# Decode attention with a gated FFN: scores keep the queries stationary on four quadrants, the softmax runs along the free axis, and one permutation matmul brings the probabilities back

## The chip, the cores and the metric

The kernel runs on one NeuronCore of a Trainium2 chip. The metric is device time in microseconds (us) of one execution. In the profile the engines are PE (TensorE, matmuls), PEld (its weight loads, which overlap with matmuls), DVE (VectorE), ACT (ScalarE), POOL (GpSimd) and SP (SyncE, which issues the loads). L371 is line 371 of the kernel before.

## The reference

One decode step for 8 sequences: attention over a sliding window of cached keys and values, multiplied by a gate from a GEGLU FFN.

```python
xn = _layernorm(x)                                   # x: 8 x 1 x 512
q  = (xn @ wq)                                       # 32 heads of 128
k  = k_cache[:, :, 3072:4096, :]                     # 8 sequences, 8 kv heads, last 1024 keys
v  = v_cache[:, :, 3072:4096, :]                     # each kv head serves 4 query heads
p  = softmax(q . k * 128 ** -0.5)                    # over the 1024 keys
s  = (p . v).reshape(B, 1, 4096) @ wo                # 4096 -> 512
g  = silu((gelu(xn @ w_gate) * (xn @ w_up)) @ w_down)
out = x + s * g
```

All inputs are bf16: 47.4 MB are read (33.6 MB of keys and values, 4.2 MB each of `wq` and `wo`, 5.5 MB of FFN weights), and 8 KB are written.

## The kernel before

**Groups and sets.** A group is one sequence with one kv head: 1024 keys, 1024 values, 4 query heads. There are 64 groups, in 16 sets of four (`QG = 4`; the four groups of a set are four sequences with the same kv head). One load brings the keys of a set, one the values, 1 MB each, so that partition e*4+g holds 32 keys of group g that lie next to each other in memory: each partition reads 8 KB in one piece, and every 128-key column block c has 32 keys of each of the four groups, interleaved on the partitions.

**Loads.** All loads are issued by SP in the order written (L159 to L173): FFN weights, `wq`, the keys of `LAG = 2` sets, and then for each set q the keys of set q+2, the values of set q and, for every second set, 0.5 MB of `wo`. They go into a ring of 16 buffers of 1 MB (`wo` has its own space). SP issues a load when its buffer is free.

**Before the sets.** The layernorm, the FFN and the query projection run while the first keys are on their way; `keep_busy` puts in matmuls that nobody reads, to keep TensorE working.

**One set.** The order on every engine is the order in which the program is written (L508 to L531). The loop runs over q (sets) and i (the four quarters of a set). In quarter i it emits the transpositions of the next quarter (`transposes`, L364: eight 128x128 blocks of K to PSUM, then two copies to SBUF, five blocks by VectorE, L371, and three by ScalarE, L373), the scores of this quarter (`scores`, L393: eight matmuls with kT as the stationary operand and the 16 query columns of the set as the moving one; each key meets the queries of all four groups, and the mask matmul L382 puts -1e30 on the three that are not its own), and a quarter of the values of set v = q - `LAG` (`values`, L472).

**Softmax before.** Scores lie as keys on partitions, 32 column blocks x 16 queries on the free axis. The maximum over a set's keys takes a reduction over blocks (L404), a transposition on TensorE (L412), a second reduction (L414), two small operations that put the negated maximum in two bf16 parts on a diagonal (L419, L422), and a matmul that adds it to all scores (L433). ScalarE takes the exponential (L442) and writes `pT`, keys on partitions, as the values need it. The sums over keys are eight matmuls with ones (L447), a reduction (L455) and a reciprocal (L461). `normalise` (L483) scales the output of a set.

**End.** `project` (L498) multiplies four heads by their part of `wo` for each second set; the last four heads come after the loop, followed by the gate, four transpositions, the addition of x, and the store.

PSUM has eight banks: two for K's transposition, two for scores, one each for maxima, sums, values and the rest.

Of the kernel before, what the change touches and what calls it, by code (L numbers as in the profile page):

```python
# [9 lines left out]
ALU = mybir.AluOpType  # L10
# [7 lines left out]
def kernel(  # L18
# [28 lines left out]

    nc = tc.nc
# [21 lines left out]
    AC = 3  # L70
# [4 lines left out]
    QC = QG * rep  # L75
    SH = B // QG
    LAG = 2
# [7 lines left out]
    p_pool = ctx.enter_context(tc.tile_pool(name="p_pool", bufs=4))  # L85
    small = ctx.enter_context(tc.tile_pool(name="small", bufs=2))
    ps_misc = ctx.enter_context(tc.tile_pool(name="ps_misc", bufs=1, space=PSUM))
    ps_kT = ctx.enter_context(tc.tile_pool(name="ps_kT", bufs=2, space=PSUM))
    ps_sc = ctx.enter_context(tc.tile_pool(name="ps_sc", bufs=2, space=PSUM))
    ps_mx = ctx.enter_context(tc.tile_pool(name="ps_mx", bufs=1, space=PSUM))  # L90
    ps_sum = ctx.enter_context(tc.tile_pool(name="ps_sum", bufs=1, space=PSUM))
# [5 lines left out]
    qT_all = persist.tile([P, B, Hq], BF16, name="qT_all")  # L97
# [70 lines left out]
    for q in range(NQ):  # L168
# [23 lines left out]
    nc.vector.memset(ones_pp, 1.0)  # L192

    row_of = consts.tile([QG, P // QG, QG], BF16, name="row_of")
    nc.vector.memset(row_of, 0.0)
    nc.gpsimd.affine_select(
        out=row_of,
        in_=row_of,
# [3 lines left out]
        pattern=[[0, P // QG], [1, QG]],  # L202
        channel_multiplier=-1,
    )
    other = consts.tile([QG, QG, rep], BF16, name="other")
    nc.vector.memset(other, MASK)
    nc.gpsimd.affine_select(
        out=other,
        in_=other,
        compare_op=ALU.not_equal,  # L210
        fill=0.0,
        base=0,
        pattern=[[1, QG], [0, rep]],
        channel_multiplier=-1,
    )

    LO = 32
    diag = []
    for i in range(2):
        t = consts.tile([LO + QC, QC], BF16, name=f"diag{i}")  # L220
        nc.vector.memset(t, 0.0)
        diag.append(t)
# [131 lines left out]
    nc.vector.tensor_copy(out=qT_all, in_=qT_ps.rearrange("p h b -> p b h"))  # L354


    kT, sc, pT, mxs, shift, recip = {}, {}, {}, {}, {}, {}

    def transposes(g):
# [9 lines left out]
        own = (NSC - AC) * P  # L369
        ta = kT_pool.tile([P, own], BF16, name="kTa")  # L370
        nc.vector.tensor_copy(out=ta, in_=kT_ps[:, 0:own])  # L371
        tb = kT_pool.tile([P, W - own], BF16, name="kTb")
        nc.scalar.copy(out=tb, in_=kT_ps[:, own:])  # L373
        kT[g] = [ta[:, c * P : (c + 1) * P] for c in range(NSC - AC)]
        kT[g] += [tb[:, c * P : (c + 1) * P] for c in range(AC)]

    def scores(g):
        q, i = divmod(g, NB)
        hkv, b = divmod(q * QG, B)
        if i == 0:  # L380
            sc[q] = ps_sc.tile([P, NCS, QC], FP32, name="sc_ps")
            nc.tensor.matmul(  # L382
                sc[q],
                row_of.rearrange("g e s -> g (e s)"),
                other.rearrange("g s j -> g (s j)")
                .unsqueeze(1)
                .to_broadcast([QG, NCS, QC]),
                start=True,
                stop=False,
                skip_group_check=True,  # L390
            )
        for c in range(NSC):
            nc.tensor.matmul(  # L393
                sc[q][:, i * NSC + c, :],
                kT[g][c],
                qT_all[:, b : b + QG, hkv * rep : (hkv + 1) * rep],
                start=False,
                stop=False,
                skip_group_check=True,
            )  # L400

    def max_keys(q):
        mx = small.tile([P, QC], FP32, name="mx")
        nc.vector.tensor_reduce(  # L404
            out=mx, in_=sc[q].rearrange("p c n -> p n c"), axis=AX.X, op=ALU.max
        )
        mxs[q] = mx
# [166 lines left out]
```

## Time and profile before

| what | value |
|---|---|
| time, median of 3 runs | 127.67 us (127.4 to 128.55) |
| profiled execution | 127.15 us, its span 125.4 us |
| PE / PEld / DVE / ACT busy | 109.9 / 85.5 / 64.3 / 42.3 us |
| mean granted clock of TensorE | 0.97 |
| bytes read | 47.46 MB, 378 GB/s over the span |
| first maximum of a set (L404) starts | 35.97 us |
| first matmul on keys (L364) starts | 31.33 us |

The span runs from the first to the last instruction; the measured time has 1.75 us more around it. A row of groups reads: line, engine, operation, output <- inputs, shapes, count, then busy time in all, mean ns of one, and idle time just before, with what ended it. Matmul durations include their way through the array (some 0.17 us), so matmuls that follow each other overlap in the rows; what a matmul costs on TensorE's path is the distance between starts. In the 40 slices each slice is 3.14 us.

### The profile page before, as it was taken

Reading aid. Unit: us, or ns where it says so; the run is one execution under the profiler, and the core shown is the slowest. Engines: PE = TensorE matmul, PEld = TensorE weight load, DVE = VectorE, ACT = ScalarE, POOL = GpSimd, SP = SyncE. Lnnn points to the kernel's source line nnn. Section 1 sums busy time; section 2 is a strip of 40 time slices with the busy share of each in tenths; the row PEclk is TensorE's granted clock in tenths of the full one; section 3 lists DMA queues with packets and bytes.
Section 4 is the critical chain, followed back from the end, with each engine's and each line's share of the span. In section 5 each row is a group of like instructions: output and inputs, shape, how many; then the busy total and the mean of one; then the engine's idle time right before and its main releaser. Section 6 shows DMA issues by size and latency. Waiting matters only on the chain.

```text
span 125.4 us, 4892 instructions
## 1 busy us (share of the span) xinstructions
PE 109.9 (88%) x2202; PEld 85.5 (68%) x2202; DVE 64.3 (51%) x200; ACT 42.3 (34%) x86; POOL 1.2 (1%) x7
## 2 busy tenths in 40 slices
PE   5997819897999999999997997969999998999780
PEld 1444315574777888878886876849888886788570
DVE  5200300101467767856866664744676675766531
ACT  4000500000356355453453434342536435344210
POOL 3000000000000000000000000000000000000000
PEclk9999995999999999999999999985999999999999
DMA  3999999999999999999999999999999999999600
GB/s 78 407 418 389 350 405 421 423 421 418 421 415 423 396 421 421 408 415 428 413 404 422 431 406 415 418 431 402 420 422 423 398 425 418 414 398 420 244 32 3
DMA packets 12373, 47.78 MB, mean 381 GB/s; under 512 B 816, under 2 KB 6720, under 8 KB 7744
## 3 DMA queue, kind: packets, MB, share of 16 engines
q1 hardware_dynamic: 12336, 47.46, 93.9%
q8 instruction: 17, 0.28, 0.9%
q14 instruction: 4, 0.03, 0.1%
q10 hardware_dynamic: 16, 0.01, 0.0%
HBM read 47.46 MB, written 0.01 MB: 378 GB/s over the span
## 4 chain that ended last, share of the span: by engine, by line
DMA 44%; PE 32%; SPq 9%; DVE 7%; ACT 4%; issue 2%; ACTq 0%
DMA ring_sb<-in_A_k_cache_dram 30%; DMA ring_sb<-in_A_v_cache_dram 14%; PE kT_ps L364 12%; PE o_ps L472 6%; PE sc_ps L393 6%; SPq L129 4%; DVE kTa L371 4%; ACT kTb L373 4%; SPq L143 3%; PE sc_ps L433 2%; PE sc_ps L382 2%; PE sT_ps L498 2%; PE sums_ps L447 2%; SPq L136 2%; DVE mx L404 1%
## 5 line engine op out<-in xcount | busy, mean ns | idle before, releaser
L373 ACT COPY kTb<-kT_ps 128x384 bf16<-128x384 bf16 x64 | 30.6, 479 | 55.7 <-DVE kTa L371 55.6
L371 DVE COPY kTa<-kT_ps 128x640 bf16<-128x640 bf16 x64 | 31.2, 489 | 23.3 <-PE kT_ps L364 22.7
L364 PE MATMUL kT_ps<-ident,ring_sb 128*128 128x128 bf16 x512 | 39.7, 221 | 3.0 <-DMA ring_sb<-in_A_k_cache_dram 3.0
L364 PEld LDWEIGHTS <-ring_sb 128*128 128x128 bf16 x512 | 29.7, 98 | 5.7 <-DMA ring_sb<-in_A_k_cache_dram 4.6
L472 PE MATMUL o_ps<-pT,ring_sb 128*128 128x64 bf16 (+1 forms) x512 | 24.7, 191 | 0.9 <-issue 0.7
L472 PEld LDWEIGHTS <-ring_sb 128*128 128x128 bf16 x512 | 19.1, 98 | 1.5 <-issue 0.8
L231 PE MATMUL idle_ps<-ones_w 128*128 128x512 bf16 x58 | 17.4, 434 | 1.5 <-DVE ones_w L177 1.5
L393 PEld LDWEIGHTS <-kTa 128*128 128x128 bf16 x320 | 14.8, 97 | 4.4 <-issue 2.0
L393 PE MATMUL sc_ps<-qT_all,kTa 128*128 128x16 bf16 x320 | 17.7, 171 | 0.0
L393 PE MATMUL sc_ps<-qT_all,kTb 128*128 128x16 bf16 x192 | 14.5, 171 | 1.3 <-ACT kTb L373 0.4
L393 PEld LDWEIGHTS <-kTb 128*128 128x128 bf16 x192 | 9.3, 96 | 2.9 <-ACT kTb L373 1.0
L404 DVE TENSOR_REDUCE mx<-sc_ps 128x16 f32<-128x512 f32 x16 | 10.9, 680 | 0.0
L442 ACT ACTIVATE pT<-sc_ps 128x512 bf16<-128x512 f32 x16 | 9.6, 602 | 2.4 <-PE sc_ps L433 2.4
L231 PEld LDWEIGHTS <-ones_w 128*128 128x128 bf16 x58 | 5.0, 102 | 6.3 <-issue 1.7
L433 PE MATMUL sc_ps<-diag,ones_pp 48*128 48x512 bf16 x16 | 6.2, 386 | 0.4 <-DVE diag L422 0.4
L447 PE MATMUL sums_ps<-pT,ones_pp 128*128 128x64 bf16 x128 | 6.5, 195 | 0.0
L382 PE MATMUL sc_ps<-other,row_of 4*128 4x512 bf16 x16 | 6.4, 398 | 0.0
L309 PEld LDWEIGHTS <-ring_sb 128*128 128x128 bf16 x56 | 2.3, 107 | 5.4 <-DMA ring_sb<-in_B_w_down_dram 3.8
L498 PEld LDWEIGHTS <-wo_sb 128*128 128x128 bf16 x128 | 4.3, 96 | 2.4 <-issue 2.4
L455 DVE TENSOR_REDUCE recip<-sums_ps 128x16 f32<-128x64 f32 x16 | 3.6, 224 | 4.3 <-PE sums_ps L447 4.3
L498 PE MATMUL sT_ps<-oT_all,wo_sb 128*128 128x8 bf16 x128 | 5.4, 167 | 0.3 <-DVE oT_all L483 0.3
L309 PE MATMUL fT_ps<-hT_sb,ring_sb 128*128 128x8 bf16 x56 | 2.3, 170 | 3.3 <-DMA ring_sb<-in_B_w_down_dram 3.3
(54 smaller groups left out, 58.7 us busy)
## 6 DMA issues: line engine op xcount, KB each, us to landing
ring_sb<-in_A_k_cache_dram SPq DMA_DIRECT2D x16, 1024.0 KB, 18.7
ring_sb<-in_A_v_cache_dram SPq DMA_DIRECT2D x16, 1024.0 KB, 18.6
ring_sb<-in_A_wq_dram SPq DMA_DIRECT2D x4, 1024.0 KB, 14.3
wo_sb<-in_A_wo_dram SPq DMA_DIRECT2D x8, 512.0 KB, 17.5
ring_sb<-in_B_w_gate_dram SPq DMA_DIRECT2D x2, 896.0 KB, 4.7
ring_sb<-in_B_w_up_dram SPq DMA_DIRECT2D x2, 896.0 KB, 8.1
ring_sb<-in_B_w_down_dram SPq DMA_DIRECT2D x2, 896.0 KB, 14.1
x_sb<-in_A_x_dram ACTq DMA_DIRECT2D x1, 8.0 KB
```

Source lines behind the costliest of these rows:

```text
L231: nc.tensor.matmul(idle_ps, ones_w[:, 0:P], ones_w, start=True, stop=True)
L364: nc.tensor.transpose(kT_ps[:, c * P : (c + 1) * P], k_sb[q][:, n * Dh : (n + 1) * Dh], ident,)
L371: nc.vector.tensor_copy(out=ta, in_=kT_ps[:, 0:own])
L373: nc.scalar.copy(out=tb, in_=kT_ps[:, own:])
L382: nc.tensor.matmul(sc[q], row_of.rearrange("g e s -> g (e s)"), other.rearrange("g s j -> g (s j)") .unsqueeze(1) .to_broadcast([QG, NCS, ...
L393: nc.tensor.matmul(sc[q][:, i * NSC + c, :], kT[g][c], qT_all[:, b : b + QG, hkv * rep : (hkv + 1) * rep], start=False, stop=False, skip_g ...
L404: nc.vector.tensor_reduce(out=mx, in_=sc[q].rearrange("p c n -> p n c"), axis=AX.X, op=ALU.max)
L433: nc.tensor.matmul(sc[q], ones_pp[0 : LO + QC, :], shift[q].unsqueeze(1).to_broadcast([LO + QC, NCS, QC]), start=False, stop=True, skip_gr ...
L442: nc.scalar.activation(out=pT[q], in_=sc[q], func=ACT.Exp, scale=inv_sqrt_dh)
L447: nc.tensor.matmul(sums_ps, ones_pp, pT[q][:, c * NB : (c + 1) * NB, :], start=(c == 0), stop=(c == NSC - 1),)
L472: nc.tensor.matmul(o_ps[q][:, 0:wide, :], v_sb[q][:, n * Dh : (n + 1) * Dh], pT[q][:, n : n + wide, :], start=(n == 0), stop=(n == NCS - 1 ...
L498: nc.tensor.matmul(sT_ps[0][:, d, :], wo_sb[:, h, d * P : (d + 1) * P], oT_all[:, h, :], start=(h == 0 and d == 0), stop=(h == Hq - 1), sk ...
```

## The change

- **Scores.** The queries become the stationary operand and kT the moving one. `qT_all` holds, for each set and group, 32 columns: the group's four queries and 28 zero columns. For each quarter, four matmuls (one for each group n) write to partitions 32n to 32n+31 of the score tile; each one takes every fourth column of kT, which are the keys of group n, 256 in all. A row of scores is now a query, with its 1024 keys along the free axis (two PSUM banks for a set, two sets held). Nothing has to be masked. 16 of the 128 rows are real.
- **kT copies.** A quarter's kT is copied whole by one engine: VectorE for the third quarter of each set and for the first quarter of odd sets, ScalarE for the others.
- **Softmax.** One reduction over 1024 elements gives the maximum of each row (`maxima`); one operation makes the bias for the exponential out of it, which on rows that are padding is -1e30 besides (`off`). The exponential gives 1024 elements in bf16 and the row's sum. VectorE transposes it in 32x32 squares. Three small operations make the reciprocal of the sum on its own row's column (`own_recip`), and one f32 matmul with ones brings it to all partitions (`sums`), followed by a copy.
- **Back to keys on partitions.** One matmul with a permutation matrix (`spread`) puts the 32x32 squares' rows in the order in which the values lie; ScalarE copies the result to `pT`. This happens one set later, at the beginning of its first quarter.
- **Order.** Values follow three sets after the scores instead of two (`LAG = 3`), so the loads put three sets of keys first; in each quarter values come ahead of scores. The number of bytes and of loads is the same.
- **Start.** `qT_all` is zeroed and filled by four copies instead of one; constants `perm`, `own`, `off`, `ones_f` take the place of `row_of`, `other` and `diag`.

```diff
-    LAG = 2
+    BK = NSC * QP                # QP = 32, NSC = 8, NCS = 32
+    GK = NCS * QP
+    LAG = 3
...
-    qT_all = persist.tile([P, B, Hq], BF16, name="qT_all")
+    qT_all = persist.tile([P, NQ, QG, QP], BF16, name="qT_all")
...
+    ones_f = consts.tile([P, P], FP32, name="ones_f")
+    nc.vector.memset(ones_f, 1.0)
+    nc.vector.memset(qT_all, 0.0)
+    perm = consts.tile([P, QP, QG], BF16, name="perm")      # 1 at partition e + 32 g
...
+    own = consts.tile([P, QG, rep], FP32, name="own")       # 1 at partition 32 g + j
...
+    off = consts.tile([P, 1], FP32, name="off")
+    nc.vector.tensor_reduce(out=off, in_=own, axis=AX.XY, op=ALU.max)
+    nc.vector.tensor_scalar(
+        out=off, in0=off, scalar1=-MASK, scalar2=MASK, op0=ALU.mult, op1=ALU.add
+    )
...
-    nc.vector.tensor_copy(out=qT_all, in_=qT_ps.rearrange("p h b -> p b h"))
+    for g in range(QG):
+        nc.vector.tensor_copy(
+            out=qT_all[:, :, g, g * rep : (g + 1) * rep].rearrange(
+                "p (h s) j -> p h s j", s=SH
+            ),
+            in_=qT_ps.rearrange("p (h j) (s g) -> p g h s j", j=rep, g=QG)[:, g],
+        )
...
+        kT[g] = kT_pool.tile([P, W], BF16, name="kT")
+        if i == 2 or (i == 0 and q % 2 == 1):
+            nc.vector.tensor_copy(out=kT[g], in_=kT_ps)
+        else:
+            nc.scalar.copy(out=kT[g], in_=kT_ps)
...
+        for n in range(QG):
             nc.tensor.matmul(
+                sc[q][n * QP : (n + 1) * QP, i * BK : (i + 1) * BK],
+                qT_all[:, q, n, :],
+                kT[g].rearrange("p (c e g) -> p g c e", c=NSC, g=QG)[:, n],
                 start=True,
+                stop=True,
+            )
+    def maxima(q):
+        mx = small.tile([P, 1], FP32, name="mx")
+        nc.vector.tensor_reduce(out=mx, in_=sc[q], axis=AX.X, op=ALU.max)
+        bias[q] = small.tile([P, 1], FP32, name="bias")
         nc.vector.tensor_scalar(
+            out=bias[q], in0=mx, scalar1=-inv_sqrt_dh, scalar2=off[:, 0:1],
+            op0=ALU.mult, op1=ALU.add,
+        )
     def exponentials(q):
+        p = p_pool.tile([P, GK], BF16, name="p")
+        total = small.tile([P, 1], FP32, name="total")
+        nc.scalar.activation(
+            out=p, in_=sc[q], func=ACT.Exp, scale=inv_sqrt_dh, bias=bias[q],
+            accum_out=total,
+        )
+        pq[q] = pq_pool.tile([P, NCS, QP], BF16, name="pq")
+        nc.vector.transpose(pq[q].rearrange("p c j -> p (c j)"), p)
+        nc.vector.tensor_scalar(
+            out=total, in0=total, scalar1=0.5, scalar2=None, op0=ALU.max
+        )
+        nc.vector.reciprocal(out=total, in_=total)
+        own_recip[q] = small.tile([P, QC], FP32, name="own_recip")
+        nc.vector.tensor_scalar(
+            out=own_recip[q], in0=own.rearrange("p g j -> p (g j)"),
+            scalar1=total[:, 0:1], scalar2=None, op0=ALU.mult,
+        )
+    def spread(q):
+        pT_ps = ps_kT.tile([P, NCS, QC], FP32, name="pT_ps", tag="kT_ps")
+        nc.tensor.matmul(
+            pT_ps, perm.rearrange("p e g -> p (e g)"), pq[q][:, :, 0:QC],
+            start=True, stop=True,
+        )
+        pT[q] = pT_pool.tile([P, NCS, QC], BF16, name="pT")
+        nc.scalar.copy(out=pT[q], in_=pT_ps)
     def sums(q):
+        nc.tensor.matmul(
+            sc[q][:, 0:QC], ones_f, own_recip[q], start=True, stop=True
+        )
+        recip[q] = recips.tile([P, QC], FP32, name="recip")
+        nc.vector.tensor_copy(out=recip[q], in_=sc[q][:, 0:QC])
...
         for i in range(NB):
             g = q * NB + i
+            if i == 0 and 1 <= q <= NQ:
+                maxima(q - 1)
             if g + 1 < NG:
                 transposes(g + 1)
-            if i == 1 and 1 <= q <= NQ:
-                max_all(q - 1)
+            if i == 0 and 2 <= q <= NQ + 1:
+                spread(q - 2)
+            if v >= 0:
+                values(v * NB + i)
             if g < NG:
                 scores(g)
-            if v >= 0:
-                if i == 0:
-                    sums(v)
-                values(v * NB + i)
-            if i == 2 and 1 <= q <= NQ:
+            if i == 1 and 1 <= q <= NQ:
                 exponentials(q - 1)
             if v >= SH and v % SH == 0 and i >= NB // 2:
                 for h in range(2):
                     project((v // SH - 1) * rep + (i - NB // 2) * 2 + h)
+            if i == NB - 1 and 1 <= q <= NQ:
+                sums(q - 1)
         if v >= 0:
             normalise(v)
-        if q < NQ:
-            max_keys(q)
```

## The prediction

> **What bounds the kernel now.** I read the 40 slices and the queue table first, for the pace of the loads, then the waits, then windows cut at the start of each set, and last the timeline of one set. The slices and the queue:
>
> ```profile
> GB/s 78 407 418 389 350 405 421 423 421 418 421 415 423 396 421 421 408 415 428 413 404 422 431 406 415 418 431 402 420 422 423 398 425 418 414 398 420 244 32 3
> q1 hardware_dynamic: 12336, 47.46, 93.9%
> ```
>
> The loads run at some 415 GB/s from the second slice to the 37th (3.14 us each), so nothing makes them wait. A set brings 2.36 MB (K and V of 1.05 MB each and, for every second set, 0.52 MB of `wo`), which is 5.68 us at 415 GB/s. The waits say whether the engines keep that pace, and windows cut from one mask matmul (L382) to the next say how fast a set goes when data are there; their columns are busy time and instructions of PE, weight loads, DVE, ACT and POOL, clock, DMA share and GB/s:
>
> ```profile
> PEld L364 <- DMA ring_sb<-in_A_k_cache_dram: 4.6, 6, 1.4
> ...
> 45.29:50.20 4.91, 4.86 (x109) 4.14 (x108) 3.67 (x12) 2.42 (x6) 0.00 (x0) 1.00 1.01 419
> 50.20:55.50 5.30, 5.25 (x125) 4.54 (x123) 3.85 (x12) 2.60 (x6) 0.00 (x0) 1.00 1.03 407
> ...
> 100.90:106.58 5.68, 5.24 (x112) 4.35 (x112) 3.65 (x12) 2.30 (x6) 0.00 (x0) 1.00 1.03 424
> ```
>
> With data there a set takes 4.91 us (5.30 with the output projection): TensorE is full, VectorE has 1.2 us to spare, ScalarE 2.5. That is quicker than the loads, so later sets are paced by them (5.68) and TensorE waits for K. Loads bound the middle. For the end I read half-microsecond windows and the timeline:
>
> ```profile
> 119.00:120.00 1.00, 1.00 (x35) 0.95 (x35) 0.23 (x1) 0.60 (x1) 0.00 (x0) 1.00 0.33 116
> ...
> 121.33 0.54 PE L498 MATMUL sT_ps<-oT_all,wo_sb 128*128 128x8 bf16 x16 [0.32 <-DVE oT_all L483]
> ```
>
> Bytes arrive until about 120.0 us; the last projection starts at 121.33 and the rest takes 125.4 - 121.33 = 4.07 us. However fast the engines become, the projection cannot start before 120.0, so at most 1.3 us (1.0%) can be won unless the loads themselves change. The change moves the same bytes; it only puts K one set further ahead. So the question is whether a set still takes less than 5.68 us.
>
> **The prices.** Rows used:
>
> ```profile
> L371 DVE COPY kTa<-kT_ps 128x640 bf16<-128x640 bf16 x64 | 31.2, 489 | 23.3 <-PE kT_ps L364 22.7
> L373 ACT COPY kTb<-kT_ps 128x384 bf16<-128x384 bf16 x64 | 30.6, 479 | 55.7 <-DVE kTa L371 55.6
> L404 DVE TENSOR_REDUCE mx<-sc_ps 128x16 f32<-128x512 f32 x16 | 10.9, 680 | 0.0
> L442 ACT ACTIVATE pT<-sc_ps 128x512 bf16<-128x512 f32 x16 | 9.6, 602 | 2.4 <-PE sc_ps L433 2.4
> ```
>
> VectorE: the maximum grows from 512 to 1024 elements; a 128-element reduction takes 270 ns (L414), so 1.07 ns an element: 0.680 + 512 x 1.07 = 1.23 us. A whole kT copy: L259 copies 32 elements in 175 ns, so 0.516 ns an element, 0.489 + 384 x 0.516 = 0.69. ScalarE: L284 does 112 elements in 264 ns, L442 512 in 602, so 0.845 an element; a whole kT copy is 0.479 + 640 x 0.845 = 1.02; the copy of `pT` has L442's shape, 0.60; the exponential of 1024 is 0.602 + 0.43 = 1.03, and 0.12 more for a bias read from a tile (L241, 8x1 with such a bias, took 293 ns where L321's line gives 171 for nothing) = 1.15. Its running total is not in the trace: between 0 and one smallest ACT operation, 0.20 (L321); I take 0.15. Small VectorE operations: 0.15 (L244, 8x1) for the guarded total and its reciprocal, 0.22 (L419) for the bias and for `own_recip`, 0.175 (L259) for the copy of `recip`, 0.23 (L483).
>
> **The 32x32 transposition** of `p` (1024 bf16, VectorE) is the large unknown. Bounds: 0.516 ns an element as for the bf16 copy, 0.69 us, or 1.07 as for the reduction and the f32 cast (L354: 256 in 425 ns), 1.23. Only plain bf16 copies reach the low rate in this trace, all operations that do more go at the high one; I take 1.20. (By itself: the Trainium skill, "VectorE: DVE Perf Modes", The three transpose paths, gives 311 ns for 128 columns; at one element per 0.96 GHz cycle an estimate of 1.24 for 1024, which would add 0.6 us to the total. No row here shows it.)
>
> **Part by part.** *TensorE* loses per set the mask (L382) and the shift (L433), 0.32 us of its path each, 32 score matmuls of 22 ns (0.7), eight sums (0.25) and the f32 transposition of maxima (0.11): 1.7. It gains 16 matmuls of 256 columns, 0.108 each at full rate (L231: 0.215 for 512), so 1.73 one after another, or 0.45 should four quadrants run together; the spread of 512 columns, 0.22; one f32 sum, 0.1 to 0.35. With 32 transpositions at 57 ns (1.83), 32 value matmuls at 28 (0.9) and 0.2 of projection that is 5.1 us, or 3.8. *ScalarE* per set: 2.5 kT copies (2.55), `pT` 0.60, exponential 1.30: 4.5. *VectorE*: 1.23 + 0.22 + 1.5 x 0.69 + 1.20 + 0.15 + 0.15 + 0.22 + 0.175 + 0.23 = 4.6. None is over 5.68 by itself. But in the old order VectorE never waited long for ScalarE; in the new one it does, in each set, and everything behind it in its queue waits too.
>
> VectorE's queue in one set is: maximum and bias of the set before; kT copy of group 2; **transposition, which waits for the exponential**; guard, reciprocal, `own_recip`; in every second set the kT copy of the next set's group 0; copy of `recip`, which waits for TensorE's sum; normalise; next maximum. The exponential waits for the bias. So one turn is maximum 1.23, bias 0.22, handoff 0.05, exponential 1.30, handoff 0.05, transposition 1.20, three small ones 0.52: 4.57. The kT copy of group 2 (0.69) lies under the exponential. Then either the f32 sum there and back (0.40), `recip` 0.175 and normalise 0.23, or 0.69 + 0.175 + 0.23 with the sum under the copy. With gaps of 0.03 between VectorE's rows: **5.55 or 5.87**.
>
> A second ring agrees: exponential 1.30, transposition 1.25, small ones 0.6, the f32 sum (TensorE holds the next set's transpositions behind it) 0.15, first transpositions and latency 0.62, kT copy on ScalarE 1.07, `pT` copy 0.60, next exponential: 5.6. TensorE's 5.1 fits under both, so whether quadrants overlap is worth nothing, nor is what TensorE loses. Loads pace nothing: K of the last set lands near 106 us (five units of 1.05 MB, 12.6 us, before the end, which trails off), long before it is wanted.
>
> *Start.* The zeroing of `qT_all` (1024 words; 64 take 112 ns in L179, so near 1.1 us), `ones_f` and `off`, which waits for POOL, hold `bn_stats` back by about 2.2 us. TensorE waits there for weights (0.7 us before most of L270, 2.1 before L309, 1.2 before the first K), which hides it; without that cover it would cost 2.2. Four strided copies of `qT_all` take 0.9 instead of 0.43 and end at 31 us, when K lands (31.3). The first set's copies now go mostly one after another through ScalarE: 32.0, 33.0, 34.05, a buffer's return, 35.8; scores and latency: the first maximum begins at 36.5 (now 35.97).
>
> *Sum.* From first to last maximum are 15 turns, eight of 5.55 and seven of 5.87, less 0.5 for two early ones without normalise: 85.0, so 121.5. Then maximum to `own_recip` 4.6 with gaps, sum and spread 0.55, `pT` copy 0.7, the last 32 value matmuls 1.07 (row at 119.95), normalise 0.33, projection to end 4.07: 11.4. Span 132.9. The profiled run took 127.15 us, 1.75 more than its span: 134.65, which is 7.5 more than that run. The median, 127.67, is 0.5 above it: **135.2 us**, 5.9% slower.
>
> **Rivals.** A difference below some 1% is not to be told from no change for this kernel.
>
> *The transposition is cheap* (not slower). At 0.69 us a turn is near 5.2: 36.5 + 77.4 + 10.9 = 124.8, 127.1 beside the median. Were it under 0.6, the 120.0 us of the loads decide: 124.1 + 1.75 + 0.5 = 126.4, at best 1% faster. It decides once a turn is under 5.2. For it: same type and size as the copies; a free running total gives 0.15 a turn more. Against: no DVE row that does more than copy has that rate.
>
> *TensorE becomes the bound.* The moving kT is read at every fourth element, which no row shows: between the 0.108 taken and double that, 16 x 0.108 = 1.7 us more a set. 6.8 us x 16 - 2.7 (three sets without values) + 31.3 + 11.4 = 148.8, so 151. For it: 5.1 us leaves only 0.6. Against: busy rows of TensorE follow columns alone. (By itself: the Trainium skill, "TensorEngine Tiling (Array Packing)", Key Properties, says that a change of tiling mode drains the array; with eight changes a set at this trace's 0.166 us for a lone matmul, an estimate of 1.3 us a set and of 146 in all. No row of this trace has such a change.)
>
> *The clock drops.* After 1.13 us without work at 82.7 the granted clock fell:
>
> ```profile
> 84.00:90.00 6.00, 6.00 (x115) 5.02 (x114) 3.35 (x11) 2.38 (x5) 0.00 (x0) 0.72 1.02 411
> ```
>
> That set took 6.35 us instead of 5.3. If TensorE's new waits (0.4 to 1 us, several a set) do this in every second set, a turn grows by some 0.4: 141.
>
> *Quadrants do not overlap*: TensorE 5.1 instead of 3.8, hidden, no change to the time.
>
> **Chances.** Forecast 0.57 (132 to 139); transposition cheap 0.19 (0.12 of it within 1%, 0.07 faster); clock 0.14; TensorE 0.10. Faster by over 1% 0.07, within 1% 0.12, slower by over 1% 0.81. The range 127 to 146 takes in the low bound of the transposition, the clock, and the cheaper TensorE case, and leaves out 0.15.
>
> **What would show it.** Right: turns of 5.5 to 5.9 us between maxima from start to end, VectorE waiting for the exponential in each; a transposition of 1.2 us; TensorE waiting for ScalarE's kT copies and for `own_recip`; loads done at 120 or sooner with 10 us of engine work behind them. Wrong: a transposition of 0.7 or less, loads still awaited after 60 us, 256-column score matmuls 0.2 us apart, or a clock under 0.9.

## The result, and the profile after

The changed kernel takes 134.75 us (median of 4, 134.11 to 135.25), beside 127.53 us for the kernel before on the same chip: 1.056 times as long, 95% interval 1.052 to 1.061. Its profiled execution took 134.11 us with a span of 132.3 us.

The starts of the sixteen maxima over a set's keys cut both spans into three parts:

| us | before | after | difference |
|---|---|---|---|
| start of the span to first maximum | 35.97 | 36.41 | +0.44 |
| first to last maximum (15 turns) | 80.79 | 81.32 | +0.53 |
| last maximum to the end of the span | 8.64 | 14.57 | +5.93 |
| span | 125.4 | 132.3 | +6.9 |

So the middle costs almost what it cost before, though for another reason, and nearly all of the loss lies behind the last maximum. The page of the kernel after, its row of GB/s and the chain that ended last:

```profile
GB/s 108 405 419 374 363 419 421 416 416 426 409 426 426 395 432 419 406 416 429 419 405 417 426 397 430 424 407 417 422 426 401 427 425 397 424 219 17 5 0 2
PE 50%; ACT 17%; DMA 14%; SPq 9%; DVE 6%; issue 2%; ACTq 0%
```

The same chain in the kernel before:

```profile
DMA 44%; PE 32%; SPq 9%; DVE 7%; ACT 4%; issue 2%; ACTq 0%
```

A slice is now 3.31 us. The loads keep their 415 GB/s and are done in the 36th slice, at about 119 us; the last four slices, 13 us, move next to nothing. In the chain, DMA is only the wait for the first keys. ScalarE, with 17%, belongs to it now. The waits of the kernel after (total us, times, longest) say the same for the keys:

```profile
PE kT_ps L379 <- ACT kT L388: 4.8, 14, 0.6
...
PEld L379 <- DMA ring_sb<-in_A_k_cache_dram: 0.9, 1, 0.9
```

Keys are awaited once, at 31 us. In their place TensorE's transpositions wait 14 times for a copy by ScalarE. The groups of the kernel after (busy us, mean ns of one, idle just before and what ended it) hold the prices, the ones that answer to the rows shown of before:

```profile
L388 ACT COPY kT<-kT_ps 128x1024 bf16<-128x1024 bf16 x40 | 40.3, 1013 | 29.8 <-PE kT_ps L379 29.7
L428 DVE STREAM_TRANSPOSE pq<-p 128x1024 bf16<-128x1024 bf16 x16 | 19.9, 1245 | 4.3 <-ACT p L419 4.3
```

One turn of the kernel after in the timeline (start, duration, engine, instruction), VectorE's and ScalarE's part of it from one maximum to the next, 5.34 us:

```profile
74.16 1.22 DVE L405 TENSOR_REDUCE mx<-sc_ps 128x1 f32<-128x1024 f32 x1
...
75.83 1.13 ACT L419 ACTIVATE p<-sc_ps,bias 128x1024 bf16<-128x1024 f32 x1
...
76.83 0.21 ACT L419 ACTIVATION_READ_ACCUMULATOR p<-sc_ps,bias 128x1 f32 x1
...
77.08 1.25 DVE L428 STREAM_TRANSPOSE pq<-p 128x1024 bf16<-128x1024 bf16 x1 [0.17 <-ACT p L419]
...
78.59 0.23 DVE L435 TENSOR_SCALAR own_recip<-own,total 128x16 f32<-128x16 f32 x1
78.74 0.69 DVE L386 COPY kT<-kT_ps 128x1024 bf16<-128x1024 bf16 x1
...
79.34 0.17 DVE L461 COPY recip<-sc_ps 128x16 f32<-128x16 f32 x1
79.42 0.22 DVE L481 TENSOR_TENSOR oT_all<-o_ps,recip 128x16 bf16<-128x16 f32 x1
79.50 1.22 DVE L405 TENSOR_REDUCE mx<-sc_ps 128x1 f32<-128x1024 f32 x1
```

Every step is the one foretold, but the last five rows overlap: the copy starts 0.08 us before `own_recip` ends, `recip` 0.09 before the copy ends, `normalise` 0.09 before that, the next maximum 0.14 before `normalise` ends. From the fourth turn to the fourteenth the length alternates between 5.34 or 5.35, in turns with VectorE's copy of the next set's first quarter, and 5.62 or 5.63, in turns with an output projection.

The end of the kernel after, in the same view:

```profile
122.04 0.23 DVE L435 TENSOR_SCALAR own_recip<-own,total 128x16 f32<-128x16 f32 x1
...
122.42 0.58 PE L457 MATMUL sc_ps<-own_recip,ones_f 128*128 128x16 f32 x2 [3.34 <-DVE own_recip L435]
...
123.46 0.59 ACT L453 CAST pT<-pT_ps 128x512 bf16<-128x512 f32 x1 [2.97 <-PE pT_ps L445]
123.49 1.44 PE L470 MATMUL o_ps<-pT,ring_sb 128*128 128x64 bf16 x24
...
125.88 1.77 PE L470 MATMUL o_ps<-pT,ring_sb 128*128 128x64 bf16 x32 [0.20 <-DVE oT_all L481]
...
127.97 0.57 PE L496 MATMUL sT_ps<-oT_all,wo_sb 128*128 128x8 bf16 x16 [0.32 <-DVE oT_all L481]
```

TensorE waits 3.34 us in its queue for the last `own_recip`. Behind that wait stand the values of set 14, which need nothing of it; they start at 123.49, so the last values start at 125.88, though their `pT` is there at 124.05. And the clock fell: windows of the kernel after (columns as before: busy of PE, weight loads, DVE, ACT, POOL, then clock, DMA share, GB/s) show it:

```profile
119.00:122.42 3.42, 0.08 (x4) 0.03 (x1) 1.88 (x5) 1.21 (x2) 0.00 (x0) 0.84 0.05 19
122.42:125.88 3.46, 3.19 (x51) 2.65 (x52) 0.54 (x3) 0.59 (x1) 0.00 (x0) 0.50 0.02 5
```

After 3.4 us almost without matmuls the granted clock is 0.50, and 32 value matmuls take 1.77 us instead of 1.07.

### The profile page after: what moved, and what is told of

Its sections match the earlier page's. It is cut to its first block, busy times and chain, and to the rows that moved or that the text cites. A ratio compares the mean times of both kernels' runs of the same rounds, so it can differ in the third digit from the quotient of the medians.

```text
span 132.3 us, 4114 instructions
## 1 busy us (share of the span) xinstructions
PE 110.8 (84%) x1813; PEld 79.2 (60%) x1818; DVE 74.8 (57%) x181; ACT 69.7 (53%) x94; POOL 1.2 (1%) x7
## 4 chain that ended last, share of the span: by engine, by line
PE 50%; ACT 17%; DMA 14%; SPq 9%; DVE 6%; issue 2%; ACTq 0%
PE kT_ps L379 23%; ACT kT L388 14%; DMA ring_sb<-in_A_k_cache_dram 14%; PE sc_ps L395 10%; PE o_ps L470 9%; PE sc_ps L457 4%; SPq L135 4%; SPq L149 3%; PE sT_ps L496 3%; DVE pq L428 3%; ACT p L419 3%; SPq L142 2%; DVE mx L405 1%; DVE own_recip L435 1%; DVE oT_all L481 0%
## 5 line engine op out<-in xcount | busy, mean ns | idle before, releaser
L388 ACT COPY kT<-kT_ps 128x1024 bf16<-128x1024 bf16 x40 | 40.3, 1013 | 29.8 <-PE kT_ps L379 29.7
L395 PE MATMUL sc_ps<-kT,qT_all 128*32 128x256 bf16 x256 | 25.3, 385 | 1.8 <-ACT kT L388 1.7
L386 DVE COPY kT<-kT_ps 128x1024 bf16<-128x1024 bf16 x24 | 16.5, 689 | 12.7 <-PE kT_ps L379 12.7
L428 DVE STREAM_TRANSPOSE pq<-p 128x1024 bf16<-128x1024 bf16 x16 | 19.9, 1245 | 4.3 <-ACT p L419 4.3
L405 DVE TENSOR_REDUCE mx<-sc_ps 128x1 f32<-128x1024 f32 x16 | 19.4, 1216 | 0.0
L419 ACT ACTIVATE p<-sc_ps,bias 128x1024 bf16<-128x1024 f32 x16 | 18.1, 1129 | 0.9 <-DVE bias L407 0.9
L453 ACT CAST pT<-pT_ps 128x512 bf16<-128x512 f32 x16 | 9.5, 591 | 4.2 <-PE pT_ps L445 4.2
L395 PEld LDWEIGHTS <-qT_all 128*32 128x32 bf16 x256 | 7.2, 93 | 5.4 <-issue 1.8
L457 PE MATMUL sc_ps<-own_recip,ones_f 128*128 128x16 f32 x32 | 6.4, 275 | 4.3 <-DVE own_recip L435 4.1
L445 PE MATMUL pT_ps<-pq,perm 128*128 128x512 bf16 x16 | 6.3, 392 | 0.0
```

The lines of the kernel that those rows point to most:

```text
L386: nc.vector.tensor_copy(out=kT[g], in_=kT_ps)
L388: nc.scalar.copy(out=kT[g], in_=kT_ps)
L395: nc.tensor.matmul(sc[q][n * QP : (n + 1) * QP, i * BK : (i + 1) * BK], qT_all[:, q, n, :], kT[g].rearrange("p (c e g) -> p g c e", c=NSC, ...
L405: nc.vector.tensor_reduce(out=mx, in_=sc[q], axis=AX.X, op=ALU.max)
L419: nc.scalar.activation(out=p, in_=sc[q], func=ACT.Exp, scale=inv_sqrt_dh, bias=bias[q], accum_out=total,)
L428: nc.vector.transpose(pq[q].rearrange("p c j -> p (c j)"), p)
```

## The experiments

Theories. *Two rings*: a turn is set by the VectorE–ScalarE ring (5.3 us) or by TensorE's queue with its wait for ScalarE's copy (5.3, or 5.6 with a projection), whichever is longer. *One ring*: VectorE and ScalarE alone set it. For the end: the order of the queue and the clock, against the mere length of the softmax. Turns, last maximum and end below are from each run's trace, ratios are to the kernel before with their 95% interval.

### The order at the end

After the last set the queue is written out: the values of sets 13 and 14 come before the last exponential, sum and permutation.

```diff
-    for q in range(NQ + LAG):
+    for q in range(NQ):
...
+    maxima(NQ - 1)
+    spread(NQ - 2)
+    for v in (NQ - 3, NQ - 2):
+        for i in range(NB):
+            values(v * NB + i)
+        normalise(v)
+    exponentials(NQ - 1)
+    for h in range(Hq - 2 * rep, Hq - rep):
+        project(h)
+    sums(NQ - 1)
+    spread(NQ - 1)
+    for i in range(NB):
+        values((NQ - 1) * NB + i)
+    normalise(NQ - 1)
```

> The changed kernel, with only the end written out in another order: once the last scores are done, the values of sets 13 and 14 and their normalisations go ahead of the last set's exponential, sum and spread, in TensorE's and VectorE's queues. The loop up to the last maximum stays (15 turns of 5.42 us). End theory: of the 14.6 us from the last maximum to the end, 2 to 3 us are values of set 14 that stand behind the last set's sum, and the half clock after TensorE's 3.3 us without work; the time falls from 134.75 to about 132, and the last values start within 0.3 us of their probabilities. Rival, the turns alone: the end is one chain of latencies, which the order does not shorten; 134 to 135.

Measured: 132.54 us, 1.038 (1.030 to 1.045). The turns stay at 5.42 on average; the end is 12.51 us instead of 14.57. The last values now start right after their `pT` (copied by 124.44), in the timeline of this kernel:

```profile
123.23 0.36 PE L457 MATMUL sc_ps<-own_recip,ones_f 128*128 128x16 f32 x2 [1.61 <-DVE own_recip L435]
...
124.49 1.77 PE L470 MATMUL o_ps<-pT,ring_sb 128*128 128x64 bf16 x32 [0.67 <-ACT pT L453]
```

Two microseconds of the loss were the order. The wait of 1.61 us still leaves the last values at half clock (1.77).

### The clock at the end

The same with nine matmuls that nobody reads in TensorE's two waits.

```diff
+    for _ in range(6):
+        nc.tensor.matmul(idle2, ones_w[:, 0:P], ones_w, start=True, stop=True)
     sums(NQ - 1)
     spread(NQ - 1)
+    for _ in range(3):
+        nc.tensor.matmul(idle2, ones_w[:, 0:P], ones_w, start=True, stop=True)
```

> The reordered end of the earlier run (132.5), with six matmuls that nobody reads ahead of the last sum and three ahead of the last values, so that TensorE is not idle for 1.6 us there. If the half clock is from idleness, the last 32 values take 1.07 us instead of 1.77, and the rows after them 0.2 less: 131.6. If the clock falls anyway, 132.5.

Measured: 131.48 us, 1.031 (1.026 to 1.036); the end is 11.62 us. The windows of this kernel over that time:

```profile
120.18:123.00 2.82, 2.53 (x51) 1.58 (x48) 1.76 (x5) 0.76 (x2) 0.00 (x0) 1.00 0.02 6
123.00:125.00 2.00, 1.96 (x32) 1.33 (x32) 0.17 (x1) 0.59 (x1) 0.00 (x0) 1.00 0.00 0
```

The clock stays at 1.00 there, the last 32 value matmuls take 1.07, and the end is 0.89 us shorter. What is left, 11.6 us, is the chain of the last softmax itself, 3.0 longer than the end of the kernel before.

### Half of the transposition

The output isn't the reference's: only half of the squares are transposed, and the permutation reads that half twice.

```diff
-        nc.vector.transpose(pq[q].rearrange("p c j -> p (c j)"), p)
+        nc.vector.transpose(
+            pq[q][:, 0 : NCS // 2, :].rearrange("p c j -> p (c j)"), p[:, 0 : GK // 2]
+        )
```

> The changed kernel, but only half of the 32x32 squares are transposed, and the spread reads that half twice (the other half of the probabilities is left out). VectorE has 0.53 us less in each turn, TensorE the same work. Theory of one ring (VectorE and ScalarE, as predicted): every turn shrinks by 0.5, 15 x 0.53 + 0.5 at the end = 8.5 us, to about 126. Theory of two rings (VectorE in turns without projection, TensorE's own queue in turns with it): the first kind shrinks by 0.3 until TensorE is the next, the second kind stays at 5.63: 2 to 3 us, to about 132.

Measured: 132.03 us, 1.036 (1.027 to 1.046). The row of the transposition falls from 1245 to 711 ns, but turns without projection only from 5.34 to 5.24, turns with one not at all (5.64). The end gains 1.3 us. Taking half a microsecond from every turn of the VectorE–ScalarE ring is worth 0.1 or nothing: another ring stands right behind it.

### Half of the values

Only half of the value matmuls are left, so TensorE has about 0.5 us less in a turn.

```diff
-        for c in range(NSC):
+        for c in range(NSC // 2):
```

> The changed kernel with every second half of a quarter's value matmuls left out (half of the keys in the sum over values), so TensorE has some 0.7 us less per set, VectorE and ScalarE the same work. One ring: the turns stay at 5.3 to 5.6, and only the end gains 1 us: about 133.5. Two rings: turns with projection fall from 5.63 to about 5.1, those without stay at 5.34: 7 x 0.5 + 1 = 4.5 us less, about 130.

Measured: 131.36 us, 1.031 (1.023 to 1.039). Turns with a projection fall from 5.62 to 5.32 (5.1 was expected), the others stay at 5.34. So TensorE's queue set the turns with a projection, and the VectorE–ScalarE ring the others.

### Both halves

Both edits together.

> Both of these at once (half of the squares transposed, half of the value matmuls left out). Two rings: both are now shorter, and all turns fall to 4.8 to 5.0, some 7 us, and 2 more at the end, to about 125.5, more than the two single gains together. One ring: the same as with half of the transposition alone, less 1 us at the end.

Measured: 129.07 us, 1.013 (1.006 to 1.020). Turns 5.03 and 5.31, mean 5.16. The expectation of 4.8 to 5.0 failed, and so did the one that the two edits together gain more than the two single gains added up: they gain 5.7 us, the single ones 2.7 and 3.4. Turns with a projection are as long as with half of the values alone, so they are still TensorE's. Both rings are shorter, but less than by their parts: in TensorE's queue the second transposition of a set still waits for ScalarE's copy of an earlier quarter, as TensorE's timeline of this kernel shows once a turn:

```profile
78.79 0.61 PE L379 MATMUL kT_ps<-ident,ring_sb 128*128 128x128 bf16 x8 [0.44 <-ACT kT L388]
```

That wait was 0.33 us in the kernel after. With work taken from TensorE it only grows, since the copy it waits for takes 1.01 us however early TensorE comes.

### How the score matmuls read kT

Two runs. In the first, one matmul with all 128 stationary columns takes the place of the four on quadrants in each quarter (the scores of three groups are left out). In the second, the four read adjacent columns instead of every fourth (the keys are the wrong ones).

```diff
-        for n in range(QG):
+        for n in range(1):
...
-                sc[q][n * QP : (n + 1) * QP, i * BK : (i + 1) * BK],
-                qT_all[:, q, n, :],
+                sc[q][:, i * BK : (i + 1) * BK],
+                qT_all[:, q, :, :].rearrange("p g j -> p (g j)"),
```

> The changed kernel with one score matmul per quarter in place of four: all 128 query columns as the stationary operand and the 256 keys of the first group moving (the scores of the other three groups with their own keys are left out). No 32-column tiles of the array are used. If the 0.22 us that the weight loads of the next transposition wait after each quarter's scores is the change between tile sizes, it goes: 4 x 0.2 us less for TensorE in a set, turns with projection fall from 5.63 to 5.34 (then VectorE's), others stay, 2 us in all: 132.5. If it is something else (the way through the array, a wait for kT), the 0.22 stays and the time with it: 134 to 135.

```diff
-                kT[g].rearrange("p (c e g) -> p g c e", c=NSC, g=QG)[:, n],
+                kT[g][:, n * BK : (n + 1) * BK],
```

> The changed kernel with each quadrant's 256 moving columns taken next to each other instead of every fourth (each group's queries then meet the wrong keys, mixed from four groups; the count of matmuls, columns and tiles is the same). Two readings of the 0.22 us that the transpositions' weight loads wait after a quarter's scores. Streaming at half rate (a 256-column matmul with every fourth column took 0.21 us on the path in the run with one full matmul, where 512 adjacent ones take 0.215): the wait falls to 0.11, TensorE has 0.4 us less in a set, turns with projection go from 5.63 to 5.34, 133. Change of tile size: the wait stays at 0.22 and the time at 134.7.

Measured: 133.43 us, 1.047 (1.037 to 1.057), and 133.25 us, 1.044 (1.036 to 1.053). In both, all turns from the fourth on are 5.31 to 5.35: TensorE's queue is short enough to lie under the other ring. What the scores of a quarter take on TensorE's path is the distance from their start to the next transposition; the row ahead of the scores is that of the eight value matmuls before them. In the kernel after, four strided ones on quadrants:

```profile
75.95 0.40 PE L470 MATMUL o_ps<-pT,ring_sb 128*128 128x64 bf16 x8
...
76.27 0.40 PE L395 MATMUL sc_ps<-kT,qT_all 128*32 128x256 bf16 x4
76.60 0.45 PEld L379 LDWEIGHTS <-ring_sb 128*128 128x128 bf16 x8 [0.22 <-issue]
76.60 0.62 PE L379 MATMUL kT_ps<-ident,ring_sb 128*128 128x128 bf16 x8
```

one strided one on the whole array, in the first of the two runs:

```profile
75.32 0.40 PE L470 MATMUL o_ps<-pT,ring_sb 128*128 128x64 bf16 x8
...
75.55 0.39 PE L395 MATMUL sc_ps<-kT,qT_all 128*128 128x256 bf16 x1
...
75.76 0.63 PE L379 MATMUL kT_ps<-ident,ring_sb 128*128 128x128 bf16 x8
```

and four with adjacent columns, in the second:

```profile
76.39 0.40 PE L470 MATMUL o_ps<-pT,ring_sb 128*128 128x64 bf16 x8
...
76.71 0.29 PE L395 MATMUL sc_ps<-kT,qT_all 128*32 128x256 bf16 x4
...
76.94 0.62 PE L379 MATMUL kT_ps<-ident,ring_sb 128*128 128x128 bf16 x8
```

That is 0.33, 0.21 and 0.23 us. One strided matmul of 256 columns takes 0.21 on the path, what 512 adjacent ones took in the kernel before (L231): the every-fourth read goes at half the rate. The four on quadrants start within 0.01 us of each other in the trace, and adjacent columns take only 0.10 off all four together, which is what one matmul of 256 columns gains at the full rate (0.108 instead of 0.21). So the quadrants work at the same time.

What is left over is the change between 32 and 128 stationary columns. Behind the scores, four on quadrants take 0.33 where one on the whole array takes 0.21, and 0.23 where the columns alone are 0.108: about 0.1 us more. Ahead of them, eight value matmuls take 0.33 and 0.32 us before scores on quadrants (75.95 to 76.27, 76.39 to 76.71) and 0.23 before scores on the whole array (75.32 to 75.55): about 0.1 us more again. So each change costs about 0.1 us, and the eight of a set about 0.8. The two readings of the wait of 0.22 us were each half right: about half of it is the strided read, the other half the change. (The Trainium skill, "TensorEngine Tiling (Array Packing)", Key Properties, has the array drain at a change of mode; the pauses of 0.1 us fit that. "SBUF — State Buffer", Specifications (TRN2), asks for at least two hits in a 16-byte line for full bandwidth and puts a penalty on each crossing to a new line; every fourth bf16 is two hits in 16 bytes, and the measured rate is half.)

### Values two sets later instead of three

```diff
-    LAG = 3
+    LAG = 2
```

> The changed kernel with values two sets after the scores, as before the change (LAG 2): one part undone. Values of a set then stand right behind its spread in TensorE's queue and wait for the copy of pT, which ScalarE makes after the first kT copy: TensorE loses 0.9 to 1.2 us in each turn, so turns of 6.2 to 6.5 us and, with one set less behind the last scores (1.5 us), about 145. Rival (the later values are of no use, since TensorE waits for VectorE or ScalarE anyhow): turns stay at 5.4, the end is 1 to 2 us shorter, 133.

Measured: 149.78 us, 1.175 (1.164 to 1.187), more than the 145 expected, with turns of 6.3 to 6.8 us from the second on (one of 7.6). TensorE's timeline of this kernel, the first values of a set:

```profile
76.17 0.39 PE L470 MATMUL o_ps<-pT,ring_sb 128*128 128x64 bf16 x8 [1.37 <-ACT pT L453]
```

The values stand behind the permutation and the `pT` copy of the same set, and all of TensorE's queue waits there. So in this order of the queue the third set of distance is worth some 15 us. Whether another order could do with two is not shown.

### Both rings shorter, with all of the work

`pT_ps` goes to the second half of the set's own scores instead of a bank of the transpositions; kT has five buffers; three quarters are always copied by ScalarE; transpositions and values are moved ahead of the scores (those of the last two quarters stand behind `normalise` and the projection), the sum one set later; the end as in the run with warm matmuls.

```diff
-        pT_ps = ps_kT.tile([P, NCS, QC], FP32, name="pT_ps", tag="kT_ps")
+        pT_ps = sc[q][:, GK // 2 :].rearrange("p (c j) -> p c j", c=NCS)
...
+        transposes(g + 1)
+        if q >= 2:
+            spread(q - 2)
+        if v >= 0:
+            values(v * NB)
+        transposes(g + 2)
+        if v >= 0:
+            values(v * NB + 1)
+        if q >= 2:
+            sums(q - 2)
+        if q >= 1:
+            exponentials(q - 1)
+        transposes(g + 3)
...
+        scores(g)
+        scores(g + 1)
+        if g + 4 < NG:
+            transposes(g + 4)
...
+        scores(g + 2)
+        scores(g + 3)
```

> The whole of the work, with both rings shortened by order alone: all first-quarter kT copies on ScalarE; the spread goes to the second bank of the old score tile, so the second transpositions need no kT buffer back from ScalarE; the sum's matmul comes a set later, so TensorE does not wait for own_recip; scores of two quarters stand together (two changes of tile size in a set instead of four); the end reordered and kept warm. Two rings: turns of 4.7 to 5.0 us, the last maximum at 108 to 112, and the loads (last bytes near 118 to 120) bound the end: span 124 to 126, time 126 to 127.5, level with the kernel before. One ring: turns of 5.1 at least (VectorE's chain maximum, exponential, transposition is not shorter), and 128.5 or more.

Measured: 129.28 us, 1.014 (1.010 to 1.018): turns of 5.18 and 5.54 from the fourth on, and not the time that was expected; by itself it lies where the theory of one ring had it (5.1 at least, 128.5 or more). In the waits of this kernel one is new:

```profile
PE sc_ps L457 <- ACT pT L453: 9.0, 16, 1.0
```

The sum writes into the score tile from which ScalarE still copies `pT`, and TensorE waits for that 0.56 us a set. So the next run splits `exponentials` into ScalarE's operation (`exponential`) and what VectorE does behind it (`squares`), puts the sum between the values of the third quarter and `squares`, and at the end the last set's squares ahead of the `normalise` of set 14:

```diff
-        if q >= 2:
-            sums(q - 2)
         if q >= 1:
-            exponentials(q - 1)
+            exponential(q - 1)
         transposes(g + 3)
         if v >= 0:
             values(v * NB + 2)
+        if q >= 2:
+            sums(q - 2)
+        if q >= 1:
+            squares(q - 1)
```

> The kernel with both rings shortened (129.3), two more waits moved: the sum's matmul behind the third transposition (it waited 0.64 us for the pT copy in each turn), and in the end the last set's squares ahead of the normalisation of set 14 (1 us). Two rings: turns of 4.8 to 5.1, last maximum at 110 to 112, end bound by the loads: span 124 to 125, time 126 to 127. If the turns are held by something that is not yet named: 5.2 and 128.

Measured: 128.41 us, 1.007 (1.004 to 1.009), not the 126 to 127 expected. Turns are 4.97 to 4.99 and 5.34 to 5.36 from the fourth to the ninth, so the short ones are below the 5.1 that the theory of one ring had as their least. From the tenth to the fourteenth they are 5.55 to 5.67, and TensorE waits for loads again; from its timeline:

```profile
107.51 0.62 PE L379 MATMUL kT_ps<-ident,ring_sb 128*128 128x128 bf16 x8 [0.50 <-DMA ring_sb<-in_A_k_cache_dram]
...
110.09 0.41 PE L475 MATMUL o_ps<-pT,ring_sb 128*128 128x64 bf16 x8 [0.43 <-DMA ring_sb<-in_A_v_cache_dram]
```

From there on the middle is bound by the loads, as before the change; the last maximum starts at 114.28, 2.5 us earlier than in the kernel before, and the end takes 12.0 us instead of 8.6.

### kT sorted by group in the copy

To have the score matmuls read adjacent columns, ScalarE wrote its copies of kT in the order of the groups.

```diff
-            nc.scalar.copy(out=kT[g], in_=kT_ps)
+            nc.scalar.copy(
+                out=kT[g].rearrange("p (g c e) -> p c e g", c=NSC, g=QG),
+                in_=kT_ps.rearrange("p (c e g) -> p c e g", c=NSC, g=QG),
+            )
```

> The same, with ScalarE writing its kT copies sorted by group, so that three of four quarters have adjacent moving columns. If the half rate of strided columns is the cause of 0.11 us per quarter and ScalarE writes at stride for nothing, turns with projection lose 0.2 to 0.3 more; the loads bound the end, so 126 to 126.5. If ScalarE's copy grows beyond 1.01 us, it is the bound, and the time goes up by 15 times 2.5 times the growth.

Measured: 292.04 us, 2.29 (2.28 to 2.30). The group of this kernel:

```profile
L388 ACT COPY kT<-kT_ps 128x1024 bf16<-128x1024 bf16 x48 | 222.6, 5010 | 11.6 <-PE kT_ps L379 11.6
```

The same copy, written in steps of 512 bytes, takes 5.01 us instead of 1.02. The half rate of the strided read is by far the cheaper place for the interleaving.

### Four sets of keys first

Beside the reordered kernel: one more set of keys ahead, the values one set later still, and at the end the values of sets 12 to 14 while the last softmax runs, those of 13 and 14 in banks that the transpositions no longer need.

```diff
-    LAG = 3
+    LAG = 4
...
+            if q in (NQ - 3, NQ - 2):
+                o_ps[q] = ps_kT.tile([P, VC, QC], FP32, name="o_ps", tag="kT_ps")
```

> The whole of the work, nothing left out. Edit beside the reordered kernel of 128.41 us: LAG is 4 instead of 3, so four sets of K come ahead of the first V and values follow four sets after the scores; at the end the values of sets 12 to 14 are emitted while the last softmax runs, each into a PSUM bank of its own, and the last sum stands behind three quarters of the last values instead of ahead of them. Theory 'the loads took over again, and only the longer softmax behind the last maximum costs': in the reordered kernel the turns grew from 5.17 to 5.62 us at set 9 because a set's step waits for the 28th of 32 loads (V of set 12); with four sets it waits for the 27th, one load (2.5 us) sooner. The last maximum should start at 111.7 to 112.5 us instead of 114.28, the last projection at 119 to 120.5 instead of 122.16 (bytes arrive until 118.7), and the time be 125 to 127 us, at or up to 2% under the kernel before (127.35). Rival 'the turns grow for another reason, or the last softmax chain of about 12 us can't be shortened': the last maximum stays near 114.3 and the time at 127.5 to 128.5. Rival 'the end only shifts': the last maximum comes early but the last values wait for V, projection at 121.3 as before, and the time is the same as before.

Measured: 126.83 us beside 127.36, 0.9967 (0.9935 to 0.9998), so at most 0.65% faster. All turns from the fifth on are 4.97 to 5.36, to the last; the last maximum starts at 111.12, 5.6 us earlier than before the change. Then TensorE waits for the last loads, in its timeline:

```profile
116.40 1.08 PE L478 MATMUL o_ps<-pT,ring_sb 128*128 128x64 bf16 x32 [2.48 <-DMA ring_sb<-in_A_v_cache_dram]
...
118.88 1.30 PEld L478 LDWEIGHTS <-ring_sb 128*128 128x128 bf16 x24 [0.80 <-DMA ring_sb<-in_A_v_cache_dram]
...
121.41 0.54 PE L504 MATMUL sT_ps<-oT_all,wo_sb 128*128 128x8 bf16 x16 [0.33 <-DVE oT_all L489]
```

Values of set 14 land at 116.4, those of set 15 at 118.9, and the projection starts at 121.41, where it started before the change (121.33). Not all of that is the loads. The granted clock was 1.00 up to 117.4 and on average 0.56 from 118.88 to 121.41, and 24 of the last value matmuls took 1.46 us, about as long as in the kernel after at a clock of 0.50 (1.44). From the start of the last values to the projection it took 2.53 us; from the run of 128.41 us, at full clock, 1.64 would be expected (1.39, and 0.25 for the sum that now stands among them), 0.9 less. This profiled execution took 127.69 us, 0.86 more than the median; that the faster executions kept the clock is not shown.

The middle went as the first theory said, the end of the profiled execution as the rival "the end only shifts", in part because of the clock. So the turns of the change can be hidden whole, and then there is little to win: the last values can't start before their load has landed, at 118.9.

## Why the prediction was right, point by point

It said 135.2 us and 134.75 was measured. The mechanism (waits between engines in place of the loads, and a longer end) is the one the trace shows, with one limit: the chain between VectorE and ScalarE, which was to set every turn, sets only those without a projection. TensorE's queue sets the five turns of 5.62, which have one. And two terms were off by some 3 us each, with opposite signs.

| step | predicted | measured |
|---|---|---|
| maximum, bias | 1.23, 0.22 | 1.22, 0.21 |
| exponential with its total | 1.15 + 0.15 | 1.13 + 0.21, 1.25 to the transposition |
| 32x32 transposition | 1.20 | 1.245 |
| kT copy VectorE, ScalarE; `pT` | 0.69, 1.02, 0.60 | 0.69, 1.01, 0.59 |
| first maximum | 36.5 | 36.41 |
| a turn | 5.55 or 5.87 | 5.62 or 5.34 |
| 15 turns | 85.0 | 81.3 |
| last maximum to the end | 11.4 | 14.6 |
| span | 132.9 | 132.3 |

- **"Loads pace nothing"** held: no wait for keys after the start, the loads done 13 us before the end.
- **The prices** held, the transposition among them. That row is 1.245, nearer to the 1.24 that the prediction mentions in brackets than to the 1.20 in its sum. The rival in which it is cheap is out; and the run with half of the squares, at 0.71 us close to the 0.69 of that rival, took 132.0 and not its 127.1, because TensorE's ring stands behind at 5.24 and the end is longer.
- **The turn of 5.87 was mis-sized by 0.53, and the one of 5.55 is near 5.62 by luck.** The first added 0.69, 0.175 and 0.23 for the last three VectorE operations and 0.03 for each gap. They overlap instead: the copy, `recip` and `normalise` move VectorE on by 0.60, 0.08 and 0.08. The second is TensorE's time: with half of the values the same turns took 5.32, so the chain that was added up to 5.55 takes 5.32 at most.
- **"TensorE's 5.1 fits under both" failed for the turns with a projection.** Its sum was near (transpositions 1.82, values 0.92, scores 0.85, eight changes of stationary columns 0.8, sum and spread 0.43, projection 0.43: 5.3), but by luck: 1.73 for scores one after another at full rate is what 0.85 at half rate, all quadrants at once, and the changes make together. The projection falls on every second turn and not on half of each, and 0.33 of waiting for ScalarE's kT copy comes on top: about 5.6. So "what TensorE loses is worth nothing" failed too: with half of the values these turns fell by 0.3, 1.5 us in five of them.
- **Score matmuls**: the half rate of the rival "TensorE becomes the bound" is there (0.21 for 256 columns), but quadrants work together, so a quarter costs 0.43 with both changes and not 0.84 and more. The rival's 151 is out by that overlap. The changes that its last sentences price at 0.166 us each, 1.3 in a set, are there too, at 0.1 each, 0.8 in a set.
- **The end of 11.4 (its parts add up to 11.3) was mis-sized by 3.2.** Up to `own_recip` it is 4.54 (4.6 with gaps). From there to the `pT` copy's end 1.78 instead of 1.25 (1.37 in the run with the end reordered); then 1.83 of waiting behind the values of set 14, not seen in the prediction: the wait that the change adds stands in TensorE's queue ahead of work that doesn't need it; the last values take 1.81 to `normalise` instead of 1.07, and the rest 4.33 instead of 4.07, at a clock of 0.50. Without order and clock drop the end is 11.62.
- **The clock rival** had the right mechanism in the wrong place: in the turns from 40 us on the clock stays at 1.00, at the end it falls.
- The size of the total is thus partly luck: -3.7 in the turns, +3.2 at the end, -0.1 at the start.

What stays open: the second transposition's wait for ScalarE was not removed alone, so the length of TensorE's ring without it in the kernel after (about 4.9 and 5.3) is worked out and not measured.

## What to carry to other kernels

When a change keeps all bytes and only moves work between engines, price two things apart: the turn, as the longest of all rings through every engine (with each second turn's extra work in that turn), and the chain behind the last turn, which nothing hides. At the end of a loop an in-order queue should be written out by hand: a matmul that waits for the last softmax belongs behind all work that doesn't, here worth 2.1 us, and keeping TensorE at work there another 0.9. And when every ring is shorter than the loads, the middle is free: 5.8 us fewer in the turns (74.95 instead of 80.79) gave 0.3%.

## What the runs showed of the hardware that was not expected

- A moving operand at every fourth bf16 streams at half rate (0.21 us for 256 columns), and four matmuls on quadrants with such reads still run at the same time (they start within 0.01 us, 0.33 for all four).
- Going from 128 stationary columns to quadrants of 32 and back cost about 0.1 us each way (eight value matmuls 0.33 instead of 0.23 ahead of it; 0.23 instead of 0.108 for 256 adjacent columns behind it), 0.8 in a set.
- A ScalarE copy that writes bf16 in steps of 512 bytes takes 5.01 us for 1024 elements instead of 1.02.
- In the turn shown, VectorE starts an operation 0.08 to 0.14 us before the one ahead of it ends where it doesn't need its result.
- In the turns, with a wait of 0.33 us in each, the granted clock stayed at 1.00 (110 to 116 us); it was 0.50 after a wait of 3.34 us and after one of 1.61 us, with 32 value matmuls in 1.77 us both times. After one of 2.48 us 32 still took 1.08, and the clock fell behind them.
